# A long convolution with a gated projection on one core: the last phase goes from one row a step to two rows a step

## The chip, the cores and the metric

The kernel runs on one NeuronCore of a Trainium2 chip. The metric is the time of one execution on the device in microseconds (us). TensorE (PE in the profile), VectorE (DVE), ScalarE (ACT), GpSimd (POOL) and the DMA queues each work through their own instructions in order, and meet by semaphores. Everything here is 32-bit floating point.

## The reference

For x and v of shape (4, 12800, 128) the reference makes a filter from a small MLP and an exponential window, convolves u = x·v with it along the sequence by an FFT of length 25600, multiplies the result by x, and puts this through a gated block with K = 5 taps (the second half below):

```python
    u = x * v
    Uf = np.fft.rfft(u, n=L, axis=1)
    Hf = np.fft.rfft(h_filt, n=L, axis=0)
    y = np.fft.irfft(Uf * Hf[None, :, :], n=L, axis=1)[:, :S, :]
    return (x * y).astype(np.float32)
...
    xp = np.concatenate([np.zeros((B, K - 1, D), dtype=np.float32), x], axis=1)
    for k in range(K):
        gate_pre += conv_w[k][None, None, :] * xp[:, k:k + S, :]
    gate = 1.0 / (1.0 + np.exp(-gate_pre))
    val = x @ w_val
    return (gate * val @ w_out).astype(np.float32)
```

## The kernel before

The convolution is written as small dense transforms. A first phase forms u and its transform over one index and writes it to DRAM (`a_u`), a second one does the middle transform, the product with the filter and the way back, and writes `c_y` to DRAM. The third and last phase, the one that changes, reads `c_y`, finishes the inverse transform, multiplies by x and does the gated block.

The last phase goes over 32 groups (two halves j of the sequence, 16 groups g each) of R = 4 rows. A row is `ROW` = 400 numbers in each of 128 partitions (4 batches of 100 positions). What a row needs, in order:

- **sum** (`y_sum`, L515): two matmuls of 512 columns, for the two parts c of `c_y`, give a tile `sd` of one PSUM bank.
- **copy** (`y_copy`, L522): ACT copies `sd` to `sd_sb` in SBUF.
- **transposes** (`y_trans`, L529): four 128x128 transposes of `sd_sb` into a tile `tp3` of one PSUM bank; ACT copies a part of it to `dif` (L531).
- **join** (`y_join`, L539, L540): DVE forms `yr` as sum and difference of `tp3` and `dif`; POOL multiplies by x (`xr`) into `ext` (L542), which holds 16 rows and a halo of 4 before them.
- **taps** (`tap`, L554, L557): the gate's convolution over a whole group of four rows at once, tap 0 on ACT and taps 1 to 4 on DVE, 1600 numbers per partition each; then the sigmoid on ACT (`sigmoid`, L561) into `sg`.
- **value** (`value`, L566): a matmul of 400 columns into `v_ps`, one bank.
- **gate product** (`gated`, L571): DVE multiplies `v_ps` by `sg` into `gd`.
- **projection** (`project`, L576): a matmul of 400 columns into `o_ps`, one bank.
- **output copy** (`finish`, L584): ACT copies `o_ps` into `o_sb`; after four rows a DMA, issued from ACT, takes it to DRAM.

PSUM has eight banks of 512 numbers in each partition. `sd`, `tp3`, `v_ps` and `o_ps` have two buffers of one bank each, which is all eight.

The order on each engine is that of the program text (`tc.manual_schedule()`): the loop over t, with the sums running three groups ahead (`AHEAD3`) of the taps and the values one group behind them. In each step r of a group, one row of each kind is emitted: transposes of a row whose copy was emitted `LAG` = 2 steps earlier, the value, the output copy of the projection emitted in the step before, the projection of the gate product emitted in the step before, a tap, the gate product, the join, the copy. The sums of two rows are emitted together in every second step. A tile that is asked for while its buffers are in use makes the writing instruction wait for the last reader of the oldest one.

Every fourth group the halo of a new `ext` is copied on ACT (`fill_halo`, L507 and its neighbours).

Of the kernel before, what the change touches and what calls it, by code (L numbers as in the profile page):

```python
# [29 lines left out]
R = 4  # L30
# [88 lines left out]
def tile_longconv_gate(  # L119
# [20 lines left out]
    nc = tc.nc  # L140
# [313 lines left out]
    with tc.tile_pool(name="p3", bufs=1) as p3, tc.tile_pool(name="ps3", bufs=1, space=PSUM) as ps3:  # L454
# [56 lines left out]
        def y_sum(s, r):  # L511
            ct, _ = loads3[s]
            sd = ps3.tile([128, B * D], F32, name="sd", bufs=2)
            for c in range(2):
                nc.tensor.matmul(  # L515
                    out=sd[c * N2:(c + 1) * N2], lhsT=inv[:, c], rhs=ct[c][:, r * B * D:(r + 1) * B * D],
                    start=True, stop=True)
            sds[s, r] = sd

        def y_copy(s, r):  # L520
            t = p3.tile([128, B, D], F32, name="sd_sb", bufs=3)
            nc.scalar.copy(out=t.rearrange("p b d -> p (b d)"), in_=sds.pop((s, r)))  # L522
            sds[s, r] = t

        def y_trans(s, r):
            t = sds.pop((s, r))
            tp = ps3.tile([D, B, 128], F32, name="tp3", bufs=2)
            for b in range(B):
                nc.tensor.transpose(out=tp[:, b], in_=t[:, b], identity=ident)  # L529
            dif = p3.tile([D, B, NC1], F32, name="dif", bufs=3)  # L530
            nc.scalar.copy(out=dif, in_=tp[:, :, N2:N2 + NC1])  # L531
            tps[s, r] = tp, dif

        def y_join(s, r):
            tp, dif = tps.pop((s, r))
            j, g = y_order[s]
            xr = loads3[s][1].rearrange("d (n b a) -> d n b a", n=R, b=B)[:, r]
            yr = p3.tile([D, B, N1], F32, name="yr", bufs=2)
            nc.vector.tensor_tensor(yr[:, :, 0:NC1], tp[:, :, 0:NC1], dif, op=ALU.add)  # L539
            nc.vector.tensor_tensor(yr[:, :, NC1:N1], tp[:, :, 1:NC1 - 1], dif[:, :, 1:NC1 - 1], op=ALU.subtract)  # L540
            e, r0 = place(j, g)
            nc.gpsimd.tensor_tensor(e[:, r0 + r], yr, xr, op=ALU.mult)  # L542
# [21 lines left out]
        def value(t, r):  # L564
            v_ps = ps3.tile([D, ROW], F32, name="v_ps", bufs=2)
            nc.tensor.matmul(out=v_ps, lhsT=wval, rhs=rows(t)[:, r * ROW:(r + 1) * ROW], start=True, stop=True)  # L566
            return v_ps

        def gated(t, r, v_ps):
            gd = p3.tile([D, ROW], F32, name="gd", bufs=2)  # L570
            nc.vector.tensor_tensor(gd, v_ps, gate_sg[t][:, r * ROW:(r + 1) * ROW], op=ALU.mult)  # L571
            return gd

        def project(gd):
            o_ps = ps3.tile([D, ROW], F32, name="o_ps", bufs=2)
            nc.tensor.matmul(out=o_ps, lhsT=wout, rhs=gd, start=True, stop=True)  # L576
            return o_ps

        def finish(t, r, o_ps):
            if r == 0:  # L580
# [3 lines left out]
            nc.scalar.copy(out=o_sb[:, r * ROW:(r + 1) * ROW], in_=o_ps)  # L584
            if r == R - 1:
# [6 lines left out]
        AHEAD3, NT, LAG = 3, len(groups), 2  # L592
        y_run, gd_last, o_last = [], None, None
        with tc.manual_schedule():
# [4 lines left out]
            for _ in range(WARM):  # L599
                w_ps = ps3.tile([D, 2 * D], F32, name="o_ps", bufs=2)  # L600
                nc.tensor.matmul(
                    out=w_ps, lhsT=ident, rhs=dft.rearrange("p a k -> p (a k)"), start=True, stop=True)
            for t in range(-AHEAD3, NT + 2):
# [78 lines left out]
```

## Time and profile before

| | us |
|---|---|
| three timed runs | 1241.81, 1249.56, 1248.66 |
| their median | 1248.66 |
| the profiled execution | 1245.33 |
| its span, first to last instruction | 1243.6 |
| first and last tap of the last phase on DVE start at | 856.2, 1229.9 |

The profile gives each engine's busy time, its instructions in order of time (start, duration, and what ended the idle time before it) and the granted TensorE clock as a share of full speed. A duration in the timeline includes the tail of an instruction's pipeline, so neighbours on one engine overlap a little there; the distance from one start to the next is what an instruction takes of its engine when nothing is waited for. Matmuls of 32-bit numbers show as two records each.

### The profile page before, as it was taken

Reading aid. Unit: us, or ns where it says so; the run is one execution under the profiler, and the core shown is the slowest. Engines: PE = TensorE matmul, PEld = TensorE weight load, DVE = VectorE, ACT = ScalarE, POOL = GpSimd, SP = SyncE. Lnnn points to the kernel's source line nnn. Section 1 sums busy time; section 2 is a strip of 40 time slices with the busy share of each in tenths; the row PEclk is TensorE's granted clock in tenths of the full one; section 3 lists DMA queues with packets and bytes.
Section 4 is the critical chain, followed back from the end, with each engine's and each line's share of the span. In section 5 each row is a group of like instructions: output and inputs, shape, how many; then the busy total and the mean of one; then the engine's idle time right before and its main releaser. Section 6 shows DMA issues by size and latency. Waiting matters only on the chain. (4 is left out here: it accounts for less than half of the span.)

```text
span 1243.6 us, 15440 instructions
## 1 busy us (share of the span) xinstructions
PE 1091.5 (88%) x5244; PEld 483.2 (39%) x5244; DVE 981.3 (79%) x1133; ACT 621.4 (50%) x1000; POOL 707.4 (57%) x282
## 2 busy tenths in 40 slices
PE   2578999768759999999999999878999999999886
PEld 1344666433323333333333333333444444444442
DVE  6576444567719999999999999706999899999897
ACT  1234755667642343343333333316667666766763
POOL 0000000000005899999999999806898888898890
PEclk9789999888878999999999999969999999999999
DMA  9999999999976777778778776388899999999932
GB/s 215 276 307 338 337 318 320 293 298 344 304 257 254 262 275 269 271 279 298 277 275 297 275 279 241 135 233 221 244 280 284 270 263 267 288 271 263 294 133 105
DMA packets 78151, 332.96 MB, mean 268 GB/s; under 512 B 8622, under 2 KB 9818, under 8 KB 57338
## 3 DMA queue, kind: packets, MB, share of 16 engines
q1 hardware_dynamic: 36928, 202.00, 55.0%
q10 hardware_dynamic: 41146, 129.98, 28.7%
q8 instruction: 43, 0.70, 0.2%
q14 instruction: 34, 0.28, 0.1%
HBM read 200.87 MB, written 131.07 MB: 267 GB/s over the span
## 5 line engine op out<-in xcount | busy, mean ns | idle before, releaser
L441 POOL TENSOR_TENSOR va<-va,vb 128x1024 f32<-128x1024 f32 x50 | 156.9, 3138 | 397.8 <-DVE vb L359 397.8
L542 POOL TENSOR_TENSOR ext<-yr,xr 128x400 f32<-128x400 f32 x120 | 301.1, 2511 | 55.7 <-DVE yr L540 35.8
L557 DVE SCALAR_TENSOR_TENSOR gt<-ext,cw,gt 128x1600 f32<-128x1600 f32 x128 | 241.3, 1885 | 1.1 <-ACT gt L554 1.1
L389 ACT COPY c_sb<-c_ps 128x1024 f32<-128x1024 f32 x100 | 101.3, 1013 | 274.1 <-PE c_ps L382 269.7
L354 PE MATMUL z_ps<-ld 128*64 128x512 f32 x800 | 196.7, 611 | 12.2 <-DMA ld<-a_u 12.2
L286 ACT COPY st<-fp 100x1024 f32<-100x1024 f32 x128 | 130.0, 1030 | 123.7 <-PE fp L285 46.0
L258 DVE TENSOR_TENSOR xv<-xv 114x1024 f32<-114x1024 f32 x64 | 78.4, 1224 | 116.7 <-DMA xv<-in_xv_dram 115.8
L515 PE MATMUL sd<-ld,inv 100*64 100x512 f32 x512 | 132.1, 622 | 9.8 <-DMA ld<-c_y 9.8
L576 PE MATMUL o_ps<-gd,wout 128*128 128x400 f32 x256 | 112.6, 522 | 26.3 <-ACT o_sb L584 12.0
L359 DVE TENSOR_TENSOR vb<-z_ps,h_sb 128x2048 f32<-128x2048 f32 x50 | 114.5, 2291 | 25.1 <-ACT c_sb L389 24.7
L359 DVE TENSOR_TENSOR va<-z_ps,h_sb 128x2048 f32<-128x2048 f32 x50 | 114.0, 2279 | 24.7 <-DMA ld<-a_u 24.7
L442 POOL TENSOR_TENSOR vc<-vc,vd 128x1024 f32<-128x1024 f32 x50 | 118.2, 2364 | 15.4 <-DVE vd L359 10.3
L443 POOL TENSOR_TENSOR va<-va,vb 128x1024 f32<-128x1024 f32 x50 | 118.5, 2370 | 0.0
L522 ACT COPY sd_sb<-sd 128x512 f32<-128x512 f32 x128 | 76.5, 598 | 75.3 <-PE sd L515 64.2
L382 PE MATMUL c_ps<-vc,ld 64*128 64x512 f32 x400 | 101.7, 627 | 9.2 <-DVE vc L432 8.8
L566 PE MATMUL v_ps<-ext,wval 128*128 128x400 f32 x256 | 107.6, 502 | 0.0
L354 PEld LDWEIGHTS z_ps<-ld 128*64 128x64 f32 x800 | 55.3, 139 | 118.6 <-issue 91.7
L382 PE MATMUL c_ps<-va,ld 64*128 64x512 f32 x400 | 99.4, 615 | 0.1
L285 PE MATMUL fp<-us,fsd 64*100 64x512 f32 (+1 forms) x256 | 76.9, 680 | 23.1 <-ACT st L286 21.7
L539 DVE TENSOR_TENSOR yr<-tp,dif 128x204 f32<-128x204 f32 x128 | 45.8, 358 | 61.7 <-ACT dif L531 61.6
L529 PEld LDWEIGHTS tp<-ident,sd_sb 128*128 128x128 f32 x512 | 59.8, 143 | 78.1 <-PE sd L515 49.5
L529 PE MATMUL tp<-ident,sd_sb 128*128 128x128 f32 x512 | 81.6, 285 | 3.6 <-DVE yr L540 3.6
(74 smaller groups left out, 1623.7 us busy)
## 6 DMA issues: line engine op xcount, KB each, us to landing
c_y<-c_sb ACTq DMA_DIRECT2D x100, 512.0 KB
ld<-a_u SPq DMA_DIRECT2D x49, 1024.0 KB
xv<-in_xv_dram SPq DMA_DIRECT2D x64, 768.0 KB
a_u<-st ACTq DMA_DIRECT2D x64, 768.0 KB
ld<-c_y SPq DMA_DIRECT2D x64, 768.0 KB
xr<-in_xt_dram SPq DMA_DIRECT2D x32, 800.0 KB
out_dram<-o_sb ACTq DMA_DIRECT2D x32, 800.0 KB
ld<-in_tab_w_dram SPq DMA_DIRECT2D x12, 1024.0 KB
```

The costliest lines, as they stand in the source:

```text
L286: nc.scalar.copy(out=st[:, c], in_=fp.rearrange("k j e -> k (j e)"))
L354: nc.tensor.matmul(out=z[half[h]], lhsT=wk[:, h, half[c]], rhs=a2[:, h, j], start=True, stop=True)
L359: nc.vector.tensor_tensor(out, z.rearrange("p (b d) -> p b d", d=D).unsqueeze(1).to_broadcast([128, n, B, D]), h_sb.unsqueeze(2).to_broadc ...
L382: nc.tensor.matmul(out=c_ps[:, h], lhsT=wk[half[h], 2 + c], rhs=vt[half[h], c].rearrange("p b d -> p (b d)"), start=(c == 0), stop=(c == 1))
L441: nc.gpsimd.tensor_tensor(va[:, 0:2], va[:, 0:2], vb[:, 0:2], op=ALU.add)
L442: nc.gpsimd.tensor_tensor(vc, vc, vd, op=ALU.add)
L443: nc.gpsimd.tensor_tensor(va[:, 2:4], va[:, 2:4], vb[:, 2:4], op=ALU.add)
L515: nc.tensor.matmul(out=sd[c * N2:(c + 1) * N2], lhsT=inv[:, c], rhs=ct[c][:, r * B * D:(r + 1) * B * D], start=True, stop=True)
L529: nc.tensor.transpose(out=tp[:, b], in_=t[:, b], identity=ident)
L542: nc.gpsimd.tensor_tensor(e[:, r0 + r], yr, xr, op=ALU.mult)
L557: nc.vector.scalar_tensor_tensor(gt, rows(t, k), cw[:, k:k + 1], gt, op0=ALU.mult, op1=ALU.add)
L576: nc.tensor.matmul(out=o_ps, lhsT=wout, rhs=gd, start=True, stop=True)
```

## The change

Everything in the last phase but the taps, the sigmoid and the DMAs now handles Q = 2 rows at once, in two steps q to a group where there were four steps r. `sd`, `tp3`, `v_ps` and `o_ps` become tiles of two banks with one buffer each: the same eight banks. A matmul still writes one bank, so there are as many matmuls and transposes as before; copies, joins, gate products and output copies are half as many and twice as wide. `LAG` goes from two one-row steps to one two-row step. Within a step the order changes too: the output copy stands ahead of the transposes, the join ahead of the gate product, and the second tap of a step behind them; the first tap of the next group and the sigmoid come at the end of the second step.

```diff
-            sd = ps3.tile([128, B * D], F32, name="sd", bufs=2)
+            sd = ps3.tile([128, Q, B * D], F32, name="sd", bufs=1)
+            for i in range(Q):
...
-            t = p3.tile([128, B, D], F32, name="sd_sb", bufs=3)
-            nc.scalar.copy(out=t.rearrange("p b d -> p (b d)"), in_=sds.pop((s, r)))
+            t = p3.tile([128, Q * B, D], F32, name="sd_sb", bufs=2)
+            nc.scalar.copy(out=t.rearrange("p b d -> p (b d)"), in_=sds.pop((s, q)).rearrange("p i e -> p (i e)"))
...
-            tp = ps3.tile([D, B, 128], F32, name="tp3", bufs=2)
+            tp = ps3.tile([D, Q * B, 128], F32, name="tp3", bufs=1)
...
-            v_ps = ps3.tile([D, ROW], F32, name="v_ps", bufs=2)
+            v_ps = ps3.tile([D, Q, 512], F32, name="v_ps", bufs=1)
...
-            o_ps = ps3.tile([D, ROW], F32, name="o_ps", bufs=2)
+            o_ps = ps3.tile([D, Q, 512], F32, name="o_ps", bufs=1)
...
-        AHEAD3, NT, LAG = 3, len(groups), 2
+        AHEAD3, NT, LAG = 3, len(groups), 1
...
-                for r in range(R):
+                for q in range(R // Q):
                     done = y_run.pop(0) if len(y_run) == LAG or s >= NT and y_run else None
-                    if done:
-                        y_trans(*done)
-                    v_ps = value(t - 1, r) if 0 <= t - 1 < NT else None
                     if o_last is not None:
                         finish(*o_last)
                         o_last = None
+                    if done:
+                        y_trans(*done)
+                    v_ps = value(t - 1, q) if 0 <= t - 1 < NT else None
                     if gd_last is not None:
                         o_last = gd_last[0], gd_last[1], project(gd_last[2])
                         gd_last = None
-                    if s < NT and r % 2 == 0:
-                        y_sum(s, r)
-                        y_sum(s, r + 1)
+                    if s < NT:
+                        y_sum(s, q)
                     if 0 <= t < NT:
-                        tap(t, r + 1)
-                    if r == R - 1 and 0 <= t + 1 < NT:
-                        tap(t + 1, 0)
-                    if v_ps is not None:
-                        gd_last = t - 1, r, gated(t - 1, r, v_ps)
+                        tap(t, 2 * q + 1)
                     if done:
                         y_join(*done)
+                    if v_ps is not None:
+                        gd_last = t - 1, q, gated(t - 1, q, v_ps)
                     if s < NT:
-                        y_copy(s, r)
-                        y_run.append((s, r))
-                    if r == R - 1 and 0 <= t < NT:
-                        sigmoid(t)
-                    if r == 1 and s < NT and g % EG == 0:
+                        y_copy(s, q)
+                        y_run.append((s, q))
+                    if 0 <= t < NT:
+                        tap(t, 2 * q + 2)
+                    if q == 1:
+                        if 0 <= t + 1 < NT:
+                            tap(t + 1, 0)
+                        if 0 <= t < NT:
+                            sigmoid(t)
+                    if q == 0 and s < NT and g % EG == 0:
                         fill_halo(j, g // EG)
```

On PE, in the middle of the last phase, the order before was as follows (the numbers behind a name tell one tile from another; `sd_sb_6318` is ACT's copy of `sd_6305`, `sd_sb_6288` its copy of a sum of the pair before).

```order
L515 MATMUL sd_6305<-ld_6122,inv_64 64x512 [waits PE_49]
L515 MATMUL sd_6305<-ld_6125,inv_64 64x512
L515 MATMUL sd_6308<-ld_6122,inv_64 64x512 [waits PE_49,Activation_49]
L515 MATMUL sd_6308<-ld_6125,inv_64 64x512
L529 MATMUL tp3_6320<-ident_68,sd_sb_6288 128x128 [waits DVE_49,PE_49]
L529 MATMUL tp3_6320<-ident_68,sd_sb_6288 128x128 x3
L566 MATMUL v_ps_6327<-ext_5798,wval_71 128x400 [waits Pool_49]
L576 MATMUL o_ps_6330<-gd_6312,wout_72 128x400 [waits DVE_49,Activation_49]
L529 MATMUL tp3_6353<-ident_68,sd_sb_6318 128x128 [waits DVE_49,Activation_49]
L529 MATMUL tp3_6353<-ident_68,sd_sb_6318 128x128 x3
```

And this is PE's order at the same place in the changed kernel, where `sd_sb_5963` is ACT's copy of `sd_5951`.

```order
L574 MATMUL v_ps_5945<-ext_5573,wval_71 128x400 [waits DVE_49,Pool_49]
L574 MATMUL v_ps_5945<-ext_5573,wval_71 128x400
L587 MATMUL o_ps_5948<-gd_5925,wout_72 128x400 [waits PE_49,Activation_49]
L587 MATMUL o_ps_5948<-gd_5925,wout_72 128x400
L519 MATMUL sd_5951<-ld_5807,inv_64 64x512 [waits PE_49]
L519 MATMUL sd_5951<-ld_5810,inv_64 64x512
L519 MATMUL sd_5951<-ld_5807,inv_64 64x512
L519 MATMUL sd_5951<-ld_5810,inv_64 64x512
L533 MATMUL tp3_5980<-ident_68,sd_sb_5963 128x128 [waits DVE_49,Activation_49]
L533 MATMUL tp3_5980<-ident_68,sd_sb_5963 128x128 x7
```

What moved: before, a sum's transposes came one transposing, one value and one projection later; now the instruction behind the sums is the transpose that reads the copy of these same sums.

On ACT, around the tap 0 (`gt`) and the sigmoid (`sg`), the order before was this.

```order
L522 COPY sd_sb_6205<-sd_6192 128x512 [waits PE_49]
L531 COPY dif_6212<-tp3_6207 128x204 [waits DVE_49,PE_49]
L584 COPY o_sb_6188<-o_ps_6190 128x400
L554 ACTIVATE gt_6220<-ext_5798,cw_73 128x1600 [waits Pool_49]
L522 COPY sd_sb_6228<-sd_6195 128x512
L561 ACTIVATE sg_6230<-gt_6110 128x1600 [waits DVE_49]
L531 COPY dif_6246<-tp3_6241 128x204 [waits PE_49]
L584 COPY o_sb_6188<-o_ps_6217 128x400
```

In the changed kernel the same stretch of ACT reads as follows, from the copy of the sums `sd_5951` on; `o_ps_5948` is the projection in PE's rows above, `o_ps_5994` the next one into the same buffer.

```order
L526 COPY sd_sb_5963<-sd_5951 128x1024 [waits PE_49]
L560 ACTIVATE gt_5966<-ext_5573,cw_73 128x1600
L567 ACTIVATE sg_5968<-gt_5883 128x1600 [waits DVE_49]
L595 COPY o_sb_5978<-o_ps_5948 128x800 [waits DMAHW2_49]
L535 COPY dif_5989<-tp3_5980 128x408 [waits PE_49]
L526 COPY sd_sb_6009<-sd_5997 128x1024 [waits PE_49]
L595 COPY o_sb_5978<-o_ps_5994 128x800
L599 DMA out_0_dram<-o_sb_5978 128x1600 [waits DMAHW6_49,Activation_49]
L535 COPY dif_6023<-tp3_6014 128x408 [waits PE_49]
```

What moved: tap 0 and the sigmoid now stand next to each other, between the copy of the sums and the output copy that frees `o_ps`.

More of the change, by code (lines that the diff above doesn't have):

```diff
@@ L509, in fill_halo, with y_sum @@
                 nc.scalar.copy(out=e[:, EG * R:], in_=tails[j])
-        def y_sum(s, r):
+        Q = 2
+        def y_sum(s, q):
             ct, _ = loads3[s]
-            sd = ps3.tile([128, B * D], F32, name="sd", bufs=2)
[L514 to L520, printed above, removed]
-            t = p3.tile([128, B, D], F32, name="sd_sb", bufs=3)
-            nc.scalar.copy(out=t.rearrange("p b d -> p (b d)"), in_=sds.pop((s, r)))
-            sds[s, r] = t
@@ L525, in y_trans @@
-        def y_trans(s, r):
-            t = sds.pop((s, r))
-            tp = ps3.tile([D, B, 128], F32, name="tp3", bufs=2)
-            for b in range(B):
+            sd = ps3.tile([128, Q, B * D], F32, name="sd", bufs=1)
+            for i in range(Q):
+                r = q * Q + i
+                for c in range(2):
+                    nc.tensor.matmul(
+                        out=sd[c * N2:(c + 1) * N2, i], lhsT=inv[:, c], rhs=ct[c][:, r * B * D:(r + 1) * B * D],
+                        start=True, stop=True)
@@ L529, in y_trans, with y_copy @@
+            sds[s, q] = sd
+        def y_copy(s, q):
+            t = p3.tile([128, Q * B, D], F32, name="sd_sb", bufs=2)
+            nc.scalar.copy(out=t.rearrange("p b d -> p (b d)"), in_=sds.pop((s, q)).rearrange("p i e -> p (i e)"))
+            sds[s, q] = t
+        def y_trans(s, q):
+            t = sds.pop((s, q))
+            tp = ps3.tile([D, Q * B, 128], F32, name="tp3", bufs=1)
+            for b in range(Q * B):
                 nc.tensor.transpose(out=tp[:, b], in_=t[:, b], identity=ident)
-            dif = p3.tile([D, B, NC1], F32, name="dif", bufs=3)
+            dif = p3.tile([D, Q * B, NC1], F32, name="dif", bufs=2)
@@ L541, in y_join @@
             e, r0 = place(j, g)
[L542 removed]
+            nc.gpsimd.tensor_tensor(
+                e[:, r0 + q * Q:r0 + (q + 1) * Q].rearrange("d n b a -> d (n b a)"),
+                yr.rearrange("d b a -> d (b a)"), xr, op=ALU.mult)
         def rows(t, k=HALO):
@@ L562, in sigmoid, with value, gated, finish @@
             gate_sg[t] = sg
-        def value(t, r):
-            v_ps = ps3.tile([D, ROW], F32, name="v_ps", bufs=2)
-            nc.tensor.matmul(out=v_ps, lhsT=wval, rhs=rows(t)[:, r * ROW:(r + 1) * ROW], start=True, stop=True)
-            return v_ps
-        def gated(t, r, v_ps):
-            gd = p3.tile([D, ROW], F32, name="gd", bufs=2)
-            nc.vector.tensor_tensor(gd, v_ps, gate_sg[t][:, r * ROW:(r + 1) * ROW], op=ALU.mult)
+        def value(t, q):
+            v_ps = ps3.tile([D, Q, 512], F32, name="v_ps", bufs=1)
+            for i in range(Q):
+                r = q * Q + i
+                nc.tensor.matmul(
+                    out=v_ps[:, i, 0:ROW], lhsT=wval, rhs=rows(t)[:, r * ROW:(r + 1) * ROW], start=True, stop=True)
+            return v_ps
+        def gated(t, q, v_ps):
+            gd = p3.tile([D, Q, ROW], F32, name="gd", bufs=2)
+            sg = gate_sg[t][:, q * Q * ROW:(q + 1) * Q * ROW].rearrange("d (i e) -> d i e", i=Q)
+            nc.vector.tensor_tensor(gd, v_ps[:, :, 0:ROW], sg, op=ALU.mult)
             return gd
         def project(gd):
-            o_ps = ps3.tile([D, ROW], F32, name="o_ps", bufs=2)
-            nc.tensor.matmul(out=o_ps, lhsT=wout, rhs=gd, start=True, stop=True)
-            return o_ps
-        def finish(t, r, o_ps):
-            if r == 0:
+            o_ps = ps3.tile([D, Q, 512], F32, name="o_ps", bufs=1)
+            for i in range(Q):
+                nc.tensor.matmul(out=o_ps[:, i, 0:ROW], lhsT=wout, rhs=gd[:, i], start=True, stop=True)
+            return o_ps
+        def finish(t, q, o_ps):
+            if q == 0:
                 o_sb = p3.tile([D, R * ROW], F32, name="o_sb", bufs=2)
@@ L583, in finish @@
             o_sb = outs3[t]
-            nc.scalar.copy(out=o_sb[:, r * ROW:(r + 1) * ROW], in_=o_ps)
-            if r == R - 1:
+            nc.scalar.copy(
+                out=o_sb[:, q * Q * ROW:(q + 1) * Q * ROW].rearrange("d (i e) -> d i e", i=Q), in_=o_ps[:, :, 0:ROW])
+            if q == R // Q - 1:
                 j, g = groups[t]
@@ L599, in tile_longconv_gate @@
             for _ in range(WARM):
-                w_ps = ps3.tile([D, 2 * D], F32, name="o_ps", bufs=2)
+                w_ps = ps3.tile([D, Q, 512], F32, name="o_ps", bufs=1)
                 nc.tensor.matmul(
-                    out=w_ps, lhsT=ident, rhs=dft.rearrange("p a k -> p (a k)"), start=True, stop=True)
+                    out=w_ps[:, 0, 0:2 * D], lhsT=ident, rhs=dft.rearrange("p a k -> p (a k)"), start=True, stop=True)
             for t in range(-AHEAD3, NT + 2):
```

10 lines of the change are left out of this document (5 added, 5 removed).

## The prediction

> **What bounds the kernel now.** I read the page's summary and its slices first, to see which engines are full and when.
>
> ```profile
> PE 1091.5 (88%) x5244; PEld 483.2 (39%) x5244; DVE 981.3 (79%) x1133; ACT 621.4 (50%) x1000; POOL 707.4 (57%) x282
> PE   2578999768759999999999999878999999999886
> DVE  6576444567719999999999999706999899999897
> ```
>
> The change touches only the last phase, the last 12 or so of the 40 slices, and there PE and DVE are both full. The busy time by stage says it in numbers; two earlier stretches stand with it for the clock, further down (columns: stretch, its length, busy time of PE, PEld, DVE, ACT, POOL, granted clock, DMA share, GB/s).
>
> ```profile
> 310.00:340.00 30.00, 20.63 (x85) 9.54 (x84) 22.36 (x47) 19.12 (x38) 0.00 (x0) 0.88 0.93 311
> 860.00:870.00 10.00, 7.46 (x32) 3.02 (x33) 10.00 (x14) 7.35 (x11) 9.78 (x5) 1.00 0.91 240
> 1000.00:1100.00 100.00, 95.66 (x404) 43.61 (x403) 95.19 (x133) 69.20 (x125) 84.93 (x34) 1.00 0.95 273
> 1100.00:1200.00 100.00, 94.68 (x401) 43.08 (x399) 93.98 (x134) 68.67 (x119) 86.56 (x34) 1.00 0.90 262
> ```
>
> The chain that ended last gives the beat: the sums of two rows recur on it.
>
> ```profile
> 1084.95 1.87 PE sd L515 x8
> 1090.60 1.87 PE sd L515 x8
> ...
> 1132.50 1.87 PE sd L515 x8
> ```
>
> Two rows take 5.65 us, a group 11.29 us. Four groups take 47.55 us, so a new halo adds 47.55 − 45.16 = 2.39. PE's timeline shows one such beat, from one pair of sums to the next:
>
> ```profile
> 1006.50 1.94 PE L515 MATMUL sd<-ld,inv 100*64 100x512 f32 x8
> 1008.37 0.66 PE L529 MATMUL tp<-ident,sd_sb 128*128 128x128 f32 x4
> 1008.86 0.84 PE L566 MATMUL v_ps<-ext,wval 128*128 128x400 f32 x2
> 1009.53 0.83 PE L576 MATMUL o_ps<-gd,wout 128*128 128x400 f32 x2
> 1010.21 0.60 PE L529 MATMUL tp<-ident,sd_sb 128*128 128x128 f32 x4
> 1010.64 0.84 PE L566 MATMUL v_ps<-ext,wval 128*128 128x400 f32 x2
> 1011.32 0.90 PE L576 MATMUL o_ps<-gd,wout 128*128 128x400 f32 x2
> 1012.14 1.94 PE L515 MATMUL sd<-ld,inv 100*64 100x512 f32 x8
> 1014.01 0.66 PE L529 MATMUL tp<-ident,sd_sb 128*128 128x128 f32 x4
> ```
>
> By distances from start to start, two rows are 1.87 of sums, 0.49 + 0.43 of transposes, 2 × 0.675 of values and 2 × 0.675 of projections (the second, 0.82, contains a short wait): 5.49 us of work in 5.64. DVE in the same time:
>
> ```profile
> 1008.81 1.87 DVE L557 SCALAR_TENSOR_TENSOR gt<-ext,cw,gt 128x1600 f32<-128x1600 f32 x1
> 1010.60 0.56 DVE L571 TENSOR_TENSOR gd<-v_ps,sg 128x400 f32<-128x400 f32 x1
> 1011.08 0.35 DVE L539 TENSOR_TENSOR yr<-tp,dif 128x204 f32<-128x204 f32 x1
> 1011.36 0.34 DVE L540 TENSOR_TENSOR yr<-tp,dif 128x196 f32<-128x196 f32 x1
> 1011.63 1.87 DVE L557 SCALAR_TENSOR_TENSOR gt<-ext,cw,gt 128x1600 f32<-128x1600 f32 x1
> ```
>
> That is 2.82 us a row with no gap: DVE sets the beat, and PE has 0.15 us of slack in 5.64. PE gets along so well because no copy by ACT stands in its way: each of its tiles has a second buffer.
>
> **The change, part by part.** *Fewer, wider operations on DVE.* From 196 to 400 columns a DVE operation grows from 0.27 to 0.48 us (start to start), 1.02 ns a column, so about 0.07 us of each is fixed. Three are merged in each two-row step: 0.21 saved, 5.44 instead of 5.65. This counts only while DVE sets the beat. PE keeps all its matmuls and saves nothing; ACT and POOL are not full.
>
> *The sums' copy comes to lie on PE's path.* In the new order PE's next instruction behind two rows' sums is the transpose that reads ACT's copy of just these sums, and the values and projections that could fill the time are queued behind it. ACT's rows give the prices.
>
> ```profile
> 1007.63 0.58 ACT L522 COPY sd_sb<-sd 128x512 f32<-128x512 f32 x1 [2.12 <-PE sd L515]
> 1009.67 1.65 ACT L554 ACTIVATE gt<-ext,cw 128x1600 f32<-128x1600 f32 x1
> 1011.20 0.59 ACT L522 COPY sd_sb<-sd 128x512 f32<-128x512 f32 x1
> 1011.67 1.56 ACT L561 ACTIVATE sg<-gt 128x1600 f32<-128x1600 f32 x1
> 1013.10 0.34 ACT L531 COPY dif<-tp 128x204 f32<-128x204 f32 x1
> ```
>
> Before has no copy of 1024 columns in this phase, but one from PSUM in the phase ahead of it; and it has one place where PE waited for ACT's output copy:
>
> ```profile
> L389 ACT COPY c_sb<-c_ps 128x1024 f32<-128x1024 f32 x100 | 101.3, 1013 | 274.1 <-PE c_ps L382 269.7
> 887.92 0.49 ACT L584 COPY o_sb<-o_ps 128x400 f32<-128x400 f32 x1
> 888.47 0.94 PE L576 MATMUL o_ps<-gd,wout 128*128 128x400 f32 x2 [1.28 <-ACT o_sb L584]
> 889.24 0.60 PE L529 MATMUL tp<-ident,sd_sb 128*128 128x128 f32 x4
> ```
>
> From PE to ACT: the first half of the pair of sums ended at about 1006.50 + 0.97 = 1007.47, the copy began at 1007.63, 0.16 later; behind the 1.87 of the sums I take 0.20. The copy itself takes 1.01. From ACT to PE: 888.41 to 888.47, 0.06; and the projection after that wait took 0.77 to the next start instead of 0.68, so 0.1 more for a matmul that starts cold behind a wait. PE's step becomes 5.49 + 0.20 + 1.01 + 0.06 + 0.10 = **6.86 us**, now a closed loop: sums, copy, transposes, value, projection, sums.
>
> *The single `o_ps` ties PE to tap 0 and the sigmoid.* In one of a group's two steps ACT does, between the copy and the output copy that frees `o_ps`, tap 0 (1009.67 to 1011.20: 1.53) and the sigmoid (1011.67 to 1013.10: 1.43). Counted from the copy's start: ACT is free of the copy after 0.90 (0.47 for 512 columns, and 0.85 ns for each further one, by 1.013 us against 0.58), of tap 0 after 2.43, of the sigmoid after 3.86; the output copy of 800 columns takes 0.49 + 400 × 0.85 ns = 0.83, and PE may project at 4.75. Without this PE would be there at 1.07 + 0.10 + 0.92 + 1.35 = 3.44. So this step waits 1.31 more, and 0.10 for the cold start: **8.27 us**. A group is 6.86 + 8.27 = 15.13 us against 11.29: 3.84 more, of which 2 × 1.37 is the copy and 1.41 the single `o_ps`, less the 0.31 of slack that was there.
>
> *What else could be late.* DVE has 2 × 5.44 = 10.9 us of work in 15.13: in the longer step tap 1 starts at 2.5, `dif` is there at 5.1 (0.5 behind the output copy), the join done by 6.1 and the gate product by 7.1, where the next values want `v_ps` only at 8.27 + 2.1 = 10.4; the single `v_ps` and `tp3` cost nothing while DVE has this slack. POOL's rows bound its two-row product:
>
> ```profile
> L542 POOL TENSOR_TENSOR ext<-yr,xr 128x400 f32<-128x400 f32 x120 | 301.1, 2511 | 55.7 <-DVE yr L540 35.8
> L442 POOL TENSOR_TENSOR vc<-vc,vd 128x1024 f32<-128x1024 f32 x50 | 118.2, 2364 | 15.4 <-DVE vd L359 10.3
> ```
>
> 800 columns take between 0.78 × 2.36 = 1.8 and 2 × 2.51 = 5.0 us, under every step. They matter where the halo's copy (ACT) waits for the last product: with 5.0, POOL ends at 6.1 + 5.0 = 11.1, some 3 us after the next copy's start at 8.27; the halo's copy (1.5, like tap 0) and the output copy behind it are done at about 5.4, where PE could project at 3.44: 2 us and a cold start, near the 2.39 of now. I take no change, with −1.5 to +1 for each of seven halos, −10 to +7. SP's queue keeps its order and is asked for its loads later than now.
>
> *The sum.* The full cycle of sums, taps and projections runs for 28 groups: 28 × 3.84 = 107.5. At the start of the phase the same wait of 1.37 stands in some eight steps, but there PE waits for other things already:
>
> ```profile
> 857.04 1.90 PE L515 MATMUL sd<-ld,inv 100*64 100x512 f32 x6 [1.39 <-DMA ld<-c_y]
> 863.76 0.63 PE L529 MATMUL tp<-ident,sd_sb 128*128 128x128 f32 x4 [1.35 <-DVE yr L540]
> ```
>
> So between 0 and 8 × 1.37 = 11, taken as 4. At the end only DVE's taps matter: 0. Together +111.5: from the profiled 1245.33 to 1357. The median of the runs is 3.3 above the profiled execution, which makes **1360**. If each of the three waits in a group is 0.1 longer or shorter than worked out, that is ±8; with the bounds of the halo and of the start, 1338 to 1382.
>
> **The rivals.** *The merged operations win* (not slower). If PE's wait for the copy were covered, DVE's 5.44 would fall below PE's own 5.49, and PE's work would set the beat: 56 × (5.65 − 5.49) = 9 less, 1240. It decides from the point at which a PE step without waits is possible, that is when the copy's 1.27 finds other matmuls in PE's queue; the order shows none between sums and transposes, so 3%. The Trainium skill, page "Perfetto Trace Analysis", section "Optimizing Scalar/DVE Operations", speaks for this rival: it puts about 125 ns of fixed cost on a DVE operation that reads PSUM and advises larger operations where the engine is saturated. By that figure the three merged ones would save, as an estimate, 56 × 0.375 = 21 us and give 1228 if DVE alone set the beat; the rows give 0.07, and PE's 5.49 stops it earlier.
>
> *Only the copy counts.* If tap 0 and the sigmoid did not delay the output copy (were `o_ps` free early enough), both steps would be 6.86: 28 × (13.72 − 11.29) + 4 = 72, 1320. Against it stands ACT's order; 8%.
>
> *The clock falls too.* PE's 10.98 of work in 15.13 makes it busy at 73%. Between 310 and 340, busy 69%, the granted clock was 0.88; between 860 and 870, busy 75%, it was 1.00. Were it 0.88, PE's work would take 1.5 us more a group: 42 more, 1402. The gaps here are 1.4 us at most and the nearer row is the second: 8%. The Trainium skill, page "TensorE: Matmul & The Clock Gate", section "A second HAM failure mode: psum-queue depth-cycling", describes just such a loss, a clock that swings because PE pauses often between groups of matmuls for PSUM; the stretch 860 to 870, with its pauses and its full clock, speaks against it here.
>
> **How the numbers follow.** The forecast has 78%, the three rivals 3, 8 and 8%, and 3% stay for what I don't see, mostly on the slow side. The range runs from 1328, a little under the forecast's own bounds toward the second rival, to 1390 toward the third. Changes under 1% (12 us) can't be told from none: the first rival, at −0.7%, falls there. So slower 0.96, the same 0.03, faster 0.01.
>
> **What would show it.** In the changed profile PE should sit idle for about 1.3 us ahead of the transposes in every step, waiting for the sums' copy, and another 1.3 us ahead of the projection, waiting for the output copy, in every second; the sums should come 6.9 and 8.3 us apart in turn; DVE and PE should both be busy about 73% of the last phase, at a clock near 1.00. Equal distances of 6.9 mean the second rival, a clock under 0.95 the third. The prediction is wrong if PE's transposes start without a wait.

## The result

The changed kernel takes 1351.61 us (median of six runs) where the kernel before takes 1244.18 (six runs): the ratio is 1.0837, with a 95% interval of 1.0796 to 1.0877. It is slower by about 107 us, where 111.5 were forecast. Some executions of a kernel take over 1.5% longer than its fastest; the medians here are over all runs, while ratios and intervals leave those executions out. The profiled execution took 1352.82 with a span of 1350.9. The page of the changed kernel shows both engines that were full no longer full in the last phase (the first row is the summary, then two rows of the 40 slices):

```profile
PE 1117.5 (83%) x5244; PEld 491.2 (36%) x5244; DVE 1029.6 (76%) x941; ACT 606.8 (45%) x808; POOL 517.5 (38%) x218
PE   2578999878579999999999989677777777777766
DVE  7576444667379999999999970488888888888885
```

By stretch (columns as in the prediction: length, busy time of PE, PEld, DVE, ACT, POOL, granted clock, DMA share, GB/s):

```profile
1000.00:1100.00 100.00, 75.81 (x313) 35.34 (x314) 86.33 (x67) 52.13 (x60) 24.55 (x13) 1.00 0.66 208
1100.00:1200.00 100.00, 76.74 (x319) 35.69 (x319) 86.58 (x69) 50.44 (x54) 24.64 (x14) 1.00 0.71 222
```

PE is busy 76%, and its granted clock is 1.00 in both stretches. DVE is busy 86%, not the forecast 73%, and POOL only 25% where it was 85%: both will matter. PE's timeline of the changed kernel, over the two steps of one group, shows the two waits:

```profile
1101.30 1.94 PE L519 MATMUL sd<-ld,inv 100*64 100x512 f32 x8
1104.38 1.09 PE L533 MATMUL tp<-ident,sd_sb 128*128 128x128 f32 x8 [1.14 <-ACT sd_sb L526]
1105.31 1.51 PE L574 MATMUL v_ps<-ext,wval 128*128 128x400 f32 x4
1108.05 1.61 PE L587 MATMUL o_ps<-gd,wout 128*128 128x400 f32 x4 [1.23 <-ACT o_sb L595]
1109.59 1.94 PE L519 MATMUL sd<-ld,inv 100*64 100x512 f32 x8
1112.64 1.10 PE L533 MATMUL tp<-ident,sd_sb 128*128 128x128 f32 x8 [1.11 <-ACT sd_sb L526]
```

The sums' copy holds PE up ahead of the transposes in every step, by 1.1 us; the output copy holds it up ahead of the projection in every second, by 1.23. From sums to sums this step takes 8.29 us (8.27 forecast). ACT in the same stretch of the changed kernel does just what was counted, the copy, tap 0, the sigmoid and only then the output copy:

```profile
1103.31 1.01 ACT L526 COPY sd_sb<-sd 128x1024 f32<-128x1024 f32 x1 [4.09 <-PE sd L519]
1104.22 1.63 ACT L560 ACTIVATE gt<-ext,cw 128x1600 f32<-128x1600 f32 x1
1105.75 1.53 ACT L567 ACTIVATE sg<-gt 128x1600 f32<-128x1600 f32 x1
1107.18 0.81 ACT L595 COPY o_sb<-o_ps 128x800 f32<-128x800 f32 x1
```

For a count over the whole phase I take the starts of tap 0 on ACT, one a group, from the fourth group to the thirtieth. Before:

```profile
889.38 1.67 ACT L554 ACTIVATE gt<-ext,cw 128x1600 f32<-128x1600 f32 x1
...
1201.52 1.64 ACT L554 ACTIVATE gt<-ext,cw 128x1600 f32<-128x1600 f32 x1
```

That is 26 groups in 312.1 us, 12.01 each. In the changed kernel:

```profile
906.92 1.64 ACT L560 ACTIVATE gt<-ext,cw 128x1600 f32<-128x1600 f32 x1
...
1301.16 1.63 ACT L560 ACTIVATE gt<-ext,cw 128x1600 f32<-128x1600 f32 x1
```

That is 394.2 us, 15.16 each. Most groups take 15.05 exactly (15.13 forecast, against 11.29). The difference of 107.3 between the two spans is then: 10.0 up to the first tap 0, 7.5 over the first three groups, 82.1 over these 26, and 7.7 behind them.

### The profile page after: what moved, and what is told of

Its sections match the earlier page's. It is cut to its first block, busy times and chain, and to the rows that moved or that the text cites. A ratio compares the mean times of both kernels' runs of the same rounds, so it can differ in the third digit from the quotient of the medians.

```text
span 1350.9 us, 14646 instructions
## 1 busy us (share of the span) xinstructions
PE 1117.5 (83%) x5244; PEld 491.2 (36%) x5244; DVE 1029.6 (76%) x941; ACT 606.8 (45%) x808; POOL 517.5 (38%) x218
## 5 line engine op out<-in xcount | busy, mean ns | idle before, releaser
L563 DVE SCALAR_TENSOR_TENSOR gt<-ext,cw,gt 128x1600 f32<-128x1600 f32 x128 | 299.1, 2339 | 30.2 <-ACT gt L560 29.0
L546 POOL TENSOR_TENSOR ext<-yr,xr 128x800 f32<-128x800 f32 x60 | 116.5, 1941 | 324.7 <-DVE yr L544 320.9
L526 ACT COPY sd_sb<-sd 128x1024 f32<-128x1024 f32 x64 | 64.8, 1012 | 231.5 <-PE sd L519 231.5
L587 PE MATMUL o_ps<-gd,wout 128*128 128x400 f32 x256 | 104.0, 530 | 46.3 <-ACT o_sb L595 46.2
L533 PE MATMUL tp<-ident,sd_sb 128*128 128x128 f32 x512 | 71.6, 284 | 75.7 <-ACT sd_sb L526 69.0
L519 PE MATMUL sd<-ld,inv 100*64 100x512 f32 x512 | 128.5, 624 | 0.0
L533 PEld LDWEIGHTS tp<-ident,sd_sb 128*128 128x128 f32 x512 | 56.3, 144 | 133.5 <-ACT sd_sb L526 129.4
L285 PE MATMUL fp<-us,fsd 64*100 64x512 f32 (+1 forms) x256 | 81.4, 717 | 28.0 <-ACT st L286 27.9
L574 PE MATMUL v_ps<-ext,wval 128*128 128x400 f32 x256 | 100.1, 515 | 3.6 <-DVE gd L581 3.6
L543 DVE TENSOR_TENSOR yr<-tp,dif 128x408 f32<-128x408 f32 x64 | 37.1, 580 | 80.0 <-ACT dif L535 80.0
```

The lines of the kernel that those rows point to most:

```text
L519: nc.tensor.matmul(out=sd[c * N2:(c + 1) * N2, i], lhsT=inv[:, c], rhs=ct[c][:, r * B * D:(r + 1) * B * D], start=True, stop=True)
L563: nc.vector.scalar_tensor_tensor(gt, rows(t, k), cw[:, k:k + 1], gt, op0=ALU.mult, op1=ALU.add)
L574: nc.tensor.matmul(out=v_ps[:, i, 0:ROW], lhsT=wval, rhs=rows(t)[:, r * ROW:(r + 1) * ROW], start=True, stop=True)
L587: nc.tensor.matmul(out=o_ps[:, i, 0:ROW], lhsT=wout, rhs=gd[:, i], start=True, stop=True)
```

## The experiments

Each run is compared with runs of the kernel before made beside it (medians 1249 to 1254 us; 1244 for the change), so the ratios are what compares. "A group" is the mean of the 26 groups above.

| kernel | ratio to before (95%) | a group, us |
|---|---|---|
| before | 1 | 12.01 |
| the change | 1.084 (1.080 to 1.088) | 15.16 |
| e1, early output copy | 1.045 (1.035 to 1.056) | 13.55 |
| e2, late transposes | 1.177 (1.168 to 1.185) | 19.02 |
| e3, both | 1.064 (1.055 to 1.073) | 14.35 |
| e4, two warm-up tiles | 1.078 (1.066 to 1.089) | 15.16 |
| e5, gate product first | 1.087 (1.077 to 1.096) | 15.32 |
| e6, before with join first | 1.035 (1.028 to 1.041) | 13.59 |
| e8, two rows, new orders | 1.007 (1.002 to 1.011) | 12.01 |
| e11, e8 with one wide product | 1.020 (1.013 to 1.028) | 12.33 |
| e12, e1 with values ahead | 1.036 (1.027 to 1.045) | 13.33 |
| e10, before with late halo | 0.992 (0.986 to 0.997) | 11.70 |

### e1: the output copy in the step of its projection

```diff
-                    if o_last is not None:
-                        finish(*o_last)
-                        o_last = None
                     if done:
                         y_trans(*done)
...
+                    if o_last is not None:
+                        finish(*o_last)
+                        o_last = None
                     if s < NT:
                         y_copy(s, q)
```

> The changed kernel with one thing moved: the output copy of a projection is emitted in the step of the projection itself, ahead of the sums' copy, and no longer behind tap 0 and the sigmoid. Theory (two closed loops, the sums' copy in both steps of a group and the single projection tile in one): the 1.2 us wait ahead of every second projection goes, the 1.1 us wait ahead of the transposes stays in every step, both steps take 6.8 us, a group 13.5 instead of 15.05, the time about 1310 us. Rival (the wait for the projection tile only stands in for another lateness, of VectorE or ScalarE, that shows up elsewhere once it is gone): a group stays near 15, the time above 1340 us.

Measured: 1306.23 us, every full group 13.55, as the theory said. In e1's timeline the projection follows the values with no wait, and the wait ahead of the transposes stays:

```profile
1106.27 1.09 PE L533 MATMUL tp<-ident,sd_sb 128*128 128x128 f32 x8 [1.14 <-ACT sd_sb L526]
1107.20 1.51 PE L574 MATMUL v_ps<-ext,wval 128*128 128x400 f32 x4
1108.55 1.51 PE L587 MATMUL o_ps<-gd,wout 128*128 128x400 f32 x4
```

So the single `o_ps` tied to tap 0 and the sigmoid costs 15.05 − 13.55 = 1.50 us a group, some 40 us of the loss.

### e2: the transposes behind values and projections

```diff
-                    if done:
-                        y_trans(*done)
                     v_ps = value(t - 1, q) if 0 <= t - 1 < NT else None
                     if gd_last is not None:
                         o_last = gd_last[0], gd_last[1], project(gd_last[2])
                         gd_last = None
+                    if done:
+                        y_trans(*done)
```

> The changed kernel with one thing moved: the transposes stand behind the values and projections of their step, so that the sums' copy has these to hide behind. Theory: the wait ahead of the transposes goes, but TensorE then comes to the projection earlier and waits there for the output copy behind tap 0 and the sigmoid: about 9.2 us for the long step and 6.2 for the short, a group 15.4, no gain: 1350 to 1365 us. Rival (each wait has its own price, the sums' copy 2 x 1.2 us a group whatever else waits): a group about 12.7, the time about 1285 us.

Measured: 1473.28 us, far above both. That there is no gain was the theory's; the size was neither's. Rows of e2, PE's and DVE's:

```profile
1100.32 2.91 PE L587 MATMUL o_ps<-gd,wout 128*128 128x400 f32 x4 [3.36 <-ACT o_sb L595]
1103.03 1.46 PE L533 MATMUL tp<-ident,sd_sb 128*128 128x128 f32 x8
1105.13 0.58 DVE L543 TENSOR_TENSOR yr<-tp,dif 128x408 f32<-128x408 f32 x1 [5.35 <-ACT dif L535]
1107.23 1.58 PE L574 MATMUL v_ps<-ext,wval 128*128 128x400 f32 x4 [0.87 <-DVE gd L581]
```

The projection waits 3.36 us for `o_ps`, the transposes now stand behind it, so `dif` is late, the join waits 5.35 us for it, and the gate product behind the join frees `v_ps` late for the next values, which wait 0.87. With one buffer for each tile, a wait in one place goes round all engines.

A second part of the miss is TensorE's clock. Behind the wait of 3.36 us the projection takes 2.71 from start to start, against 1.34 in the next step, which has no such wait; the transposes take 1.39 against 0.97. The long step, 11.85 here where 9.2 were forecast, is longer by 1.37 + 0.42 + 0.87. Over 1000 to 1100 the granted clock was 0.86 in e2. So part of e2's loss is a lower clock, not the order alone.

### e3: both moves

```diff
-                    if o_last is not None:
-                        finish(*o_last)
-                        o_last = None
-                    if done:
-                        y_trans(*done)
                     v_ps = value(t - 1, q) if 0 <= t - 1 < NT else None
...
+                    if o_last is not None:
+                        finish(*o_last)
+                        o_last = None
+                    if done:
+                        y_trans(*done)
                     if s < NT:
                         y_sum(s, q)
...
-                    if done:
-                        y_join(*done)
                     if v_ps is not None:
                         gd_last = t - 1, q, gated(t - 1, q, v_ps)
+                    if done:
+                        y_join(*done)
```

> Both moves together (transposes behind values and projections; the output copy in the step of its projection, ahead of the sums' copy), and the gate product ahead of the join as in the kernel before. The tiles stay as in the change, two banks and one buffer each. Theory (order, not the single buffers themselves, closes the loops): a step falls to the work of TensorE or VectorE, 5.5 to 5.8 us, a group 11.0 to 11.6, the time 1235 to 1260 us. Rival (single two-bank tiles cost whatever the order): a group above 12.5, the time above 1285 us.

Measured: 1333.08 us, a group of 14.35: the theory fell. Neither copy holds PE up any more, and it is not faster than e1. Note that e3 makes a third move, the gate product ahead of the join. In e3's rows the new bound is DVE, with POOL beside it:

```profile
1101.89 5.32 DVE L563 SCALAR_TENSOR_TENSOR gt<-ext,cw,gt 128x1600 f32<-128x1600 f32 x2
1102.05 3.48 POOL L546 TENSOR_TENSOR ext<-yr,xr 128x800 f32<-128x800 f32 x1 [3.63 <-DVE yr L544]
1108.16 1.61 PE L574 MATMUL v_ps<-ext,wval 128*128 128x400 f32 x4 [1.41 <-DVE gd L581]
```

The product starts 0.16 after a tap and takes 3.48 us: the 1.6 that the tap still runs, and 1.9. The two taps take 5.32 together instead of 2 × 1.8: 1.7 more, about the product's own time. It looks as if a tap and a product exclude each other, the one that starts first holding the other off. The two kernels' own profiles can be read so too. Before:

```profile
1003.16 1.87 DVE L557 SCALAR_TENSOR_TENSOR gt<-ext,cw,gt 128x1600 f32<-128x1600 f32 x1
1003.31 2.61 POOL L542 TENSOR_TENSOR ext<-yr,xr 128x400 f32<-128x400 f32 x1 [2.79 <-DVE yr L540]
1004.95 0.56 DVE L571 TENSOR_TENSOR gd<-v_ps,sg 128x400 f32<-128x400 f32 x1
```

and in the changed kernel, where the gate product stands between the join and the tap:

```profile
1100.96 0.98 DVE L581 TENSOR_TENSOR gd<-v_ps,sg 128x800 f32<-128x800 f32 x1
1101.12 1.89 POOL L546 TENSOR_TENSOR ext<-yr,xr 128x800 f32<-128x800 f32 x1 [4.65 <-DVE yr L544]
1101.86 2.83 DVE L563 SCALAR_TENSOR_TENSOR gt<-ext,cw,gt 128x1600 f32<-128x1600 f32 x1
```

Before, the tap starts first, and the product of 400 columns ends 0.97 us after the next DVE operation starts. In the changed kernel the product starts first, runs undisturbed in 1.89 for twice the columns, and the tap takes 2.83, 0.96 more. To test this, e6 changes the order alone, in the kernel before.

### e6: the kernel before, join ahead of the gate product

```diff
-                    if v_ps is not None:
-                        gd_last = t - 1, r, gated(t - 1, r, v_ps)
                     if done:
                         y_join(*done)
+                    if v_ps is not None:
+                        gd_last = t - 1, r, gated(t - 1, r, v_ps)
```

> The kernel before with one thing moved: the join stands ahead of the gate product, as in the changed kernel. Theory (a tap on VectorE and a product on GpSimd exclude each other, the one that starts first holds the other off): the one-row product, 1.0 us when alone, now starts together with the gate product (0.5) and holds the next tap off for 0.5 to 0.7 us; VectorE's row grows from 2.82 to 3.4 or 3.5 us, the products shrink from 2.6 to about 1.1 us, the time rises to 1300 to 1325 us. Rival (it was the wider operand that let GpSimd slow VectorE in the changed kernel): nothing moves, 1244 us within 5.

Measured: 1292.82 us, a group without halo 13.37 instead of 11.29, 0.52 more a row. The theory's direction is there and the rival's "nothing moves" is not, but the size is below the theory's: a row is 3.34 where 3.4 to 3.5 were expected, and the time lies under its 1300 to 1325. Same width, same tiles; in e6's rows the product has shrunk to 1.03 and the tap has grown to 2.39:

```profile
1040.40 0.56 DVE L571 TENSOR_TENSOR gd<-v_ps,sg 128x400 f32<-128x400 f32 x1
1040.56 1.03 POOL L542 TENSOR_TENSOR ext<-yr,xr 128x400 f32<-128x400 f32 x1 [2.31 <-DVE yr L540]
1040.89 2.39 DVE L557 SCALAR_TENSOR_TENSOR gt<-ext,cw,gt 128x1600 f32<-128x1600 f32 x1
```

So GpSimd holds VectorE off without a wider operand. The Trainium skill, page "SBUF — State Buffer", section "Who interferes with whom", has the rule: a VectorE instruction with two inputs in SBUF and a GpSimd one that reads SBUF share a port that one of them holds for its whole length, and the order of issue decides who is blocked. A tap reads `ext` and `gt` from SBUF; the join and the gate product read PSUM and one tile in SBUF, and products run beside them in all these rows. The traces agree.

### e8: two-row steps in new orders

PE does value, sums, projection, transposes; DVE tap, gate product, tap, join; the output copy stands in the step of its projection; the halo is copied in the second step; POOL multiplies one row at a time, so that a product that has waited for a tap to end fits beside the gate product or the join.

```diff
-            nc.gpsimd.tensor_tensor(
-                e[:, r0 + q * Q:r0 + (q + 1) * Q].rearrange("d n b a -> d (n b a)"),
-                yr.rearrange("d b a -> d (b a)"), xr, op=ALU.mult)
+            ev, yv = e.rearrange("d n b a -> d (n b a)"), yr.rearrange("d b a -> d (b a)")
+            for i in range(Q):
+                r = r0 + q * Q + i
+                nc.gpsimd.tensor_tensor(
+                    ev[:, r * ROW:(r + 1) * ROW], yv[:, i * ROW:(i + 1) * ROW], xr[:, i * ROW:(i + 1) * ROW], op=ALU.mult)
...
+                    v_ps = value(t - 1, q) if 0 <= t - 1 < NT else None
+                    if 0 <= t < NT:
+                        tap(t, 2 * q + 1)
+                    if q == 1 and 0 <= t + 1 < NT:
+                        tap(t + 1, 0)
+                    if s < NT:
+                        y_sum(s, q)
+                    if gd_last is not None:
+                        o_last = gd_last[0], gd_last[1], project(gd_last[2])
+                        gd_last = None
+                    if v_ps is not None:
+                        gd_last = t - 1, q, gated(t - 1, q, v_ps)
+                    if 0 <= t < NT:
+                        tap(t, 2 * q + 2)
+                    if s < NT:
+                        y_copy(s, q)
+                        y_run.append((s, q))
+                    if done:
+                        y_trans(*done)
+                    if o_last is not None:
+                        finish(*o_last)
+                        o_last = None
+                    if q == 1 and 0 <= t < NT:
+                        sigmoid(t)
+                    if done:
+                        y_join(*done)
```

> Two-row steps with the tiles of the change, all orders new: TensorE value, sums, projection, transposes; VectorE tap, gate product, tap, join; ScalarE the output copy in the step of its projection; and GpSimd's product in two products of one row, so that each fits beside the gate product or the join and no tap meets one. Theory: no loop over a copy is closed any more and no tap is held off; a group takes 11.2 to 11.4 us, the time 1215 to 1240 us. Rival (two-bank tiles with one buffer, or operations over two rows, cost something of their own): a group of 12 us or more, 1265 us or more.

Measured: 1257.78 us, 0.65% over before by the ratio, between theory and rival. Ten of its 26 groups take 11.2 to 11.3 as the theory said, the others 11.8 to 13.2. In e8's rows the sums wait for a load, and POOL's two products take 5.30 together without holding a tap off; the last row is from the table of waits from 900 to 1200 (us in total, times, longest):

```profile
1044.98 1.90 PE L519 MATMUL sd<-ld,inv 100*64 100x512 f32 x6 [0.72 <-DMA ld<-c_y]
1050.57 1.94 PE L519 MATMUL sd<-ld,inv 100*64 100x512 f32 x8
1051.07 5.30 POOL L549 TENSOR_TENSOR ext<-yr,xr 128x400 f32<-128x400 f32 x2 [2.08 <-DVE yr L544]
1056.20 1.94 PE L519 MATMUL sd<-ld,inv 100*64 100x512 f32 x8
PEld sd L519 <- DMA ld<-c_y: 15.1, 13, 1.8
```

So tiles of two banks with one buffer are not slow in themselves: in another order nearly all of the 8.4% is gone. The longer groups go with late loads: from 900 to 1200 the sums of e8 wait 15.1 us on PEld and 4.4 on PE for loads of `c_y`, and its 25 or so groups there are some 19 us longer than at 11.25; the kernel before, the change and e11 show no such wait. The loads of `c_y` (L115) stand on SP's queue behind the load of `xr`, which waits until POOL's product has freed its buffer; with 5.30 for two rows POOL may well be what makes them late. No run tests that.

### e11: e8 with one product of two rows

```diff
-            ev, yv = e.rearrange("d n b a -> d (n b a)"), yr.rearrange("d b a -> d (b a)")
-            for i in range(Q):
...
+            nc.gpsimd.tensor_tensor(
+                e[:, r0 + q * Q:r0 + (q + 1) * Q].rearrange("d n b a -> d (n b a)"),
+                yr.rearrange("d b a -> d (b a)"), xr, op=ALU.mult)
```

> The kernel e8 with the one difference that GpSimd's product is one of two rows as in the change. Theory (exclusion of taps and products): the product, 1.9 us alone, no longer fits beside the gate product or the join, each holds a tap off by about 0.9 us; a group takes 12 to 13.5 us, the time 1255 to 1290 us. Rival (the width doesn't matter): as e8.

Measured: 1274.34 us, 1.3% above e8, most groups 12.1 to 12.6. The grouped rows of e11 (count, busy time and mean in ns) show taps at 2241 ns and products at 3451:

```profile
L563 DVE SCALAR_TENSOR_TENSOR gt<-ext,cw,gt 128x1600 f32<-128x1600 f32 x98 | 219.6, 2241 | 0.0
L546 POOL TENSOR_TENSOR ext<-yr,xr 128x800 f32<-128x800 f32 x46 | 158.7, 3451 | 127.0 <-DVE yr L544 112.6 <-PE sd L519 14.4
```

The joins and gate products leave room for two products of 1.0 one at a time, not for one of 1.9. And since e11 has the product of the change, its 1.020 against 1.084 is what the orders alone are worth.

### e12: e1 with the values ahead of the transposes

```diff
-                    if done:
-                        y_trans(*done)
                     v_ps = value(t - 1, q) if 0 <= t - 1 < NT else None
+                    if done:
+                        y_trans(*done)
```

> The kernel e1 (early output copy) with the values ahead of the transposes, so that the sums' copy (1.2 us) has the values (1.35 us) to hide behind. Theory one (TensorE's loop over the sums' copy alone sets the 13.55 us of e1): the wait of 1.1 us goes, a step falls to VectorE's 6.4 us with its held-off taps, a group to 12.8 to 13.0, the time to 1280 to 1290 us. Theory two (VectorE, ScalarE and TensorE have grown into one loop there: transposes, their copy, join, gate product, and back to the values, with the tap held off by the product): the wait only moves, to the values or the join, a group stays at 13.4 to 13.8 and the time at 1300 to 1312 us.

Measured: 1297.75 us, a ratio of 1.036 where e1 has 1.045, the intervals overlapping; a group 13.3, a little under the second theory's 13.4 to 13.8 and above the first one's 13.0. The second is the nearer: the wait ahead of the transposes is gone, and one of the same size stands ahead of the values (e12's rows):

```profile
1111.82 1.58 PE L574 MATMUL v_ps<-ext,wval 128*128 128x400 f32 x4 [1.09 <-DVE gd L581]
1113.24 1.04 PE L533 MATMUL tp<-ident,sd_sb 128*128 128x128 f32 x8
```

The copy's wait is real in the changed kernel and in e1, but behind it stands a DVE step of about 6.6 us with its held-off taps, so that hiding the copy alone brings little.

### e5: the changed kernel, gate product ahead of the join

```diff
-                    if done:
-                        y_join(*done)
                     if v_ps is not None:
                         gd_last = t - 1, q, gated(t - 1, q, v_ps)
+                    if done:
+                        y_join(*done)
```

> The changed kernel with one thing moved: the gate product stands ahead of the join, as in the kernel before. Theory (taps and products exclude each other, but VectorE has slack in the changed kernel): the product now meets two taps in a row, takes 3.4 us instead of 1.9 and holds the second tap off by 1.6 us, and the time stays at 1351 us within 10, since TensorE's two loops still set the pace. Rival (the join's place was part of the loss): 20 us or more either way.

Measured: 1362.27 us, ratio 1.087 against 1.084: the same within the intervals. In e5's rows the product has grown to 3.47, and PE waits for `o_ps` as before the move:

```profile
1108.23 3.47 POOL L546 TENSOR_TENSOR ext<-yr,xr 128x800 f32<-128x800 f32 x1 [3.97 <-DVE yr L544]
1114.17 1.61 PE L587 MATMUL o_ps<-gd,wout 128*128 128x400 f32 x4 [1.23 <-ACT o_sb L595]
```

The second of two taps is now held off by 1.6 us instead of 0.96, and a group without a halo stays at 15.05. So the exclusion is in the changed kernel, but DVE has slack there and PE's two loops cover it.

### e4: warm-up matmuls on two tiles

```diff
-                w_ps = ps3.tile([D, Q, 512], F32, name="o_ps", bufs=1)
+                w_ps = ps3.tile([D, Q, 512], F32, name=("o_ps", "v_ps")[_ % 2], bufs=1)
```

> The changed kernel; only the 18 warm-up matmuls ahead of the last phase write two tiles in turn instead of one tile with one buffer. Theory: they took 23 us instead of 9.8 because each waited for the end of the one before, and the first sums came 5 to 9 us late for it; with two tiles they take about 10 us, the first sums come when their loads land, the time falls by 5 to 8 us to about 1345 us. Rival (the first sums wait for loads anyway, or the colder clock at the start takes it back): the time stays at 1351 us.

Inconclusive: 1355.88 us, ratio 1.078, not to be told from the change. In its profile the 18 warm-up matmuls take 9.7 us, as with two buffers in the kernel before. The one-tile form takes 23.0 in the profiles of the change, e3, e5, e11 and e12, at a granted clock of 0.50 from 820 to 840, and 13.6 in those of e1, e2 and e8, at 0.83 or more from 810 to 830. So of the 13 us about 4 belong to the tile and some 9 come with the lower clock; whether writing one tile brings that clock on is open.

### e10: the kernel before with the halo copied later

```diff
-                    if r == 1 and s < NT and g % EG == 0:
+                    if r == R - 1 and s < NT and g % EG == 0:
```

> The kernel before with the halo copies two steps later in their group. Theory (the 2.4 us that a halo costs before is ScalarE waiting for the last product while its other copies are queued behind): the cost goes nearly, 13 to 17 us less, about 1230 us. Rival (it is the copy's own time on ScalarE): 1244 us within 5.

Measured: 1249.78 us beside 1253.50, ratio 0.992 with an interval of 0.986 to 0.997. It is the one kernel of these that may beat both, by under 1%. The firmer sign is in the profile: a group with a halo mostly takes 12.37 instead of 13.52, so half of the extra cost is gone. That is less than the theory's whole cost and more than the rival's nothing, and what keeps the other half is open.

## Why the prediction was right

**The bound and the two loops: right.** PE's waits stand where they were put. The step with the copy alone was 6.86 forecast and is 15.05 − 8.29 = 6.76; the one with the output copy 8.27 and 8.29. e1 takes the second loop away and both steps become 6.78, the group 13.55, against 13.72 worked out for the rival that only the copy counts. That rival's condition did not hold in the change, and its price was right.

**"The merged operations win": the saving was right, the step that made it a bound was wrong.** DVE's rows in the changed kernel:

```profile
1108.49 0.58 DVE L543 TENSOR_TENSOR yr<-tp,dif 128x408 f32<-128x408 f32 x1 [0.72 <-ACT dif L535]
1108.99 0.55 DVE L544 TENSOR_TENSOR yr<-tp,dif 128x392 f32<-128x392 f32 x1
1109.47 0.98 DVE L581 TENSOR_TENSOR gd<-v_ps,sg 128x800 f32<-128x800 f32 x1
1110.37 4.75 DVE L563 SCALAR_TENSOR_TENSOR gt<-ext,cw,gt 128x1600 f32<-128x1600 f32 x2
1115.04 0.58 DVE L543 TENSOR_TENSOR yr<-tp,dif 128x408 f32<-128x408 f32 x1
```

Join and gate product take 1.88 from start to start where two rows of them took 2 × 1.03: 0.18 saved by three merges, against the 0.21 worked out and 0.375 by the Trainium skill's figure (page "Perfetto Trace Analysis", section "Optimizing Scalar/DVE Operations"), which this trace does not bear out. But "5.44 instead of 5.65" took the taps as unchanged. They took 4.67 for two, not 3.58, since a wide product held one off: DVE's step was 6.55. With the copies' waits covered, DVE still needs 6.6 a step in e12 and 7.1 in e3, more than the 5.65 of before; 1240 was not to be had by covering the waits alone. And in e8's short groups, where neither a copy nor a load holds PE up, PE takes 5.63 from sums to sums (1050.57 to 1056.20 in e8's rows) and not the 5.49 of the rival, so that next to nothing was to be won on 5.65. The bounds of POOL's product, 1.8 to 5.0, were worked out without asking why 400 columns had taken 2.5 and 1024 only 2.4.

**The sum came out because errors offset each other.** The 26 groups: 26 × (15.05 − 11.29) = 97.8, as forecast but for 0.08 a group. *Halo*: taken as no change, bounded by −10; beyond 11.29 a group, the groups with a halo or a new half add 18.6 to these 26 before, and beyond 15.05 they add 2.9 in the changed kernel, so −15.7, outside the bound. The product that the halo's copy waits for took 1.9, close to the lower bound, not the 5.0 that was taken; in e5, where it takes 3.47, they add 7.0. *Start*: taken as 4, bounded by 11. The 17.5 measured up to the fourth tap 0 hold two full groups that the forecast has among its 28 (7.1 there, 7.7 forecast), so the start itself is 10.5, just within its bound. The fill's transposes did wait 1.1 to 1.2 us in each of the first six steps; what was not on the list at all are the warm-up matmuls, which also write `o_ps`. Before:

```profile
810.67 9.79 PE L601 MATMUL o_ps<-dft,ident 128*128 128x256 f32 x36 [1.10 <-ACT c_sb L389]
826.20 1.94 PE L515 MATMUL sd<-ld,inv 100*64 100x512 f32 x2 [5.75 <-DMA ld<-c_y]
```

and in the changed kernel, where the first sums no longer wait for their load:

```profile
812.26 22.98 PE L613 MATMUL o_ps<-dft,ident 128*128 128x256 f32 x36 [1.10 <-ACT c_sb L389]
835.17 3.68 PE L519 MATMUL sd<-ld,inv 100*64 100x512 f32 x8
```

Of the 10.5, 1.6 lies ahead of the warm-up, and that is scatter: the program up to there is the same in all twelve kernels, and their profiles have the warm-up start anywhere from 810.7 to 826.9. Most of the 13 us that the warm-up grew by goes with the lower clock of this execution (see e4), so the size of this term is partly luck.

*End*: taken as 0, measured 7.7. Behind the last sums the projections still wait for the output copy, by 1.9 and 2.4 us in these two rows of the changed kernel:

```profile
1317.08 3.04 PE L587 MATMUL o_ps<-gd,wout 128*128 128x400 f32 x4 [1.91 <-ACT o_sb L595]
1327.06 2.44 PE L587 MATMUL o_ps<-gd,wout 128*128 128x400 f32 x4 [2.40 <-ACT o_sb L595]
```

Together 97.8 − 15.7 + 17.5 + 7.7 = 107.3. The group's 3.76 was understood; that the rest adds up to so little is luck.

**"The clock falls too": did not happen in the full groups.** With PE busy 76% and waits of 1.1 to 1.2 us, the granted clock was 1.00, as the stretch from 860 to 870 had said. At the start of the phase it was 0.50 from 820 to 840, against 0.72 and 0.59 in these two stretches before. And e2 shows that the rival was a real one: with waits of 3.36 us and PE busy 70%, the clock was 0.86 from 1000 to 1100.

## What to carry to other kernels

Joining operations in pairs while PSUM stays the same size spends the second buffer, and then the order of the instructions must supply what the buffer did: between a matmul and the matmul that reads its evacuated copy, and between an output copy and the next write of its tile, there must be other work on both engines. Walk each single-buffered tile round its loop, through every queue, and write down what stands ahead of the release; that gave what a group lost (3.76 us, 3.84 forecast) to within about 2%. Hiding one wait of several in such a ring can take it away (e1) or only move it (e12), or make it worse (e2).

## What the runs showed of the hardware

A tap on VectorE and a product on GpSimd, both with two inputs in SBUF, run one after the other and not side by side, and the first to start wins. A product of 400 columns takes 1.03 us alone and 2.61 if a tap starts 0.15 ahead of it; one of 800 columns 1.89 and 3.48; a tap takes 1.87, and 2.39, 2.83 or about 3.4 us if a product is ahead of it. The kernel before sits in a narrow place here: its product of 1.0 us just fits beside a join and a gate product of 1.03 together, and moving two instructions past each other on VectorE (e6) costs 3.5%.

TensorE's matmuls ran slower behind the longest waits. Behind 3.36 us without a matmul (e2) four projection matmuls took 2.91 us; behind 1.23 us (the changed kernel) they took 1.61, and 1.51 with no wait. In 1000 to 1100 the granted clock was 0.86 in e2 and 1.00 in the changed kernel. How long a wait has to be is not shown: at the end of the changed kernel they took 3.04 us behind a wait of 1.91.
